# A causal convolution and a Fourier layer on one core: full-height products in the second stage, and other buffers first for the mixing weights

## The chip, the cores and the metric

The kernel runs on one core of a Trainium2 chip. The metric is the device time of one execution in microseconds. Engines are named as in the profile: PE is TensorE (PEld its weight loads), DVE VectorE, ACT ScalarE, POOL GpSimd, SP SyncE.

## What is computed

`x` is 8 batches x 3264 rows x 192 channels (f32). First a causal convolution of 7 taps with softmaxed weights for each of 8 heads; its result is the `x` of the second part, a Fourier layer: the lowest 64 frequencies along the rows are mixed over the channels with complex matrices, transformed back and added to `x`, and then a small matrix product with a relu is added.

```python
out = np.einsum('hk,bskhg->bshg', w, x_unf)          # convolution, w = softmax(weight)
x = out.reshape(B, S, D)
...
X = np.fft.rfft(x, axis=1)                            # n_modes = 64
Yr = np.einsum('bmd,mde->bme', Xr, w_r) - np.einsum('bmd,mde->bme', Xi, w_i)
Yi = np.einsum('bmd,mde->bme', Xr, w_i) + np.einsum('bmd,mde->bme', Xi, w_r)
y = np.fft.irfft(Y, n=S, axis=1)
u = x + y
return (u + np.maximum(u @ w_ch, 0.0)).astype(np.float32)
```

## The kernel before, in words

The 8 batches form four pairs (`q` = 0 to 3). The convolved rows lie in `xall` (bf16) in slots of 128 rows of both batches of a pair: 25 whole slots and one of half tiles per pair. The order of the work on each engine is the order in which the program writes it; engines wait for each other by semaphores.

**First stage.** For each unit of four or five slots: convolution (`conv`, products of 64 rows and 64 columns of the array, L285), copies back to `xall` (L303, L305), and the product with the sine and cosine table `ftab` (`dft_unit`, full height, L311). Between them TensorE transposes the rows into `cm` (channels 0 to 127, `cm_bank`, L360) and `ct` (channels 128 to 191, two batches on the two halves of the partitions, `ct_bank`, L371); both are views of the tile `cc`, which has four quarters, one for each pair. `some(n)` does the next `n` of these banks from the list `tjobs`.

**Mixing.** 16 groups of four frequencies. `mix(g)` is 12 products (L428), each on a quarter of the array's columns, with the weights of group `g`. The weights come by GpSimd's queue (`load_w`, L417: two DMAs of 288 KB a group, for w_r and w_i). Nine groups have a place before the mixing starts: four in the last quarter of `cc`, which is still free, and five in the `arena`. `wbuf(g)` gives groups 0 to 3 the quarter of `cc` and 4 to 8 the arena; group `g` from 9 on goes where `g - 5` lay, and is loaded when `mix(g - 5)` is done. After each second group ScalarE copies the result out (`mix_copy`, L435), and TensorE transposes it (`mix_trans`, L441) into `yet` (copies L446, L448). Between the groups stand transposes of `ftab` and of the last quarter; those that write the last quarter of `cc` come after the groups whose weights lie there. The PSUM banks of the second stage's first two tiles (`za`) are taken after group 13, and the c products of the first two duos (`first_c`) run behind groups 13 and 14.

**Between.** `yet` is multiplied with `wm` and `w1` (L587, L588), which gives `zw`, the mixed frequencies with and without `w_ch`, for the first four batches; those of the others come in two items of the second stage (`zw_batch`, L505, L506).

**Second stage.** 53 items: 50 duos of two slots, one duo of half tiles ("h") and two items of `zw_batch`. Four PSUM tiles of two banks take turns (`za`, `zb`). What a duo adds up in PSUM:

- c: the rows times `w_ch`, from `cm` with `wm` and from `ct` with `wt2` (which holds the lower 64 rows of `w_ch` on both halves of the partitions);
- g: `ftab` times the part of `zw` that has `w_ch` in it; then a relu in place on ScalarE (`relu`, L521);
- y: `ftab` times the other part of `zw`; then VectorE adds `xall` (`finish`, L540) and SyncE stores the result (L549, 384 KB a duo).

`both` issues c, g or y for the two units of a duo side by side: one unit on rows 0 to 63 of the array, the other on rows 64 to 127, each into its own bank, and later with the halves exchanged. A bank takes the other half only when the first is done: `turn` puts a wait there. One duo has 20 products of half height, all at L499. An item `n` of the loop issues c and g of the first half for `n`, y of the second half for `n - 2` with its add and store, c and g of the second half for `n` and its relu, and y of the first half for `n - 1`.

Of the kernel before, what the change touches and what calls it, by code (L numbers as in the profile page):

```python
# [19 lines left out]
def kernel(  # L20
# [32 lines left out]
    def sb(name, shape, dtype, **kw):  # L53
# [5 lines left out]
    NW = 5  # L59
# [363 lines left out]
    def mix(g):  # L423
        yp = low[(g // 2) % 2][:, D * (g % 2):D * (g % 2) + D]
        for j in range(3):
            for p4 in range(4):
                m = 4 * g + p4
                nc.tensor.matmul(yp[32 * p4:32 * p4 + 2 * B, :], xt[:, j, :, m],  # L428
                                 wbuf(g)[:, p4, j, :], start=(j == 0), stop=(j == 2),
                                 tile_position=(0, 32 * p4), skip_group_check=True)  # L430
        if g >= NL:
            load_w(g + NW)

    def mix_copy(d):
        nc.scalar.copy(out=ymix[d % 2][:], in_=low[d % 2][:, 0:2 * D].rearrange("p (g d) -> p g d", g=2))  # L435

    def mix_trans(d):
        ets = [low[2 + t][:, :].bitcast(BF16)[:, 0:2 * P].rearrange("p (g k) -> p g k", g=2) for t in range(2)]
        for t in range(2):
            for g in range(2):  # L440
                nc.tensor.transpose(ets[t][:, g, :], ymix[d % 2][:, g, 64 * t:64 * t + P], ident[:])  # L441
        for t in range(2):
            dst = yet[:, t, :, :].rearrange("p (c m) b -> p m c b", c=2)[:, 8 * d:8 * d + 8, :, :]
            srcv = ets[t].rearrange("p g (q k) -> p (g q) k", q=4)[:, :, 0:16].rearrange("p m (c b) -> p m c b", c=2)
# [11 lines left out]
    some(2)  # L456


    def z_pieces(u, row, which):

        r = slice(64 * row, 64 * row + 64)
        res = []
        if u[0] == "h":
            for k, q in enumerate(u[1]):
                cols = slice(D * k, D * k + D)
                if which == "c":
                    res.append((cols, cm[r, q, 2 * NF, :], wm[r, 0:D]))
                    res.append((cols, ct[r, q, NF, :], wt2[r, :]))
                else:
                    for i in range(2):  # L470
                        res.append((cols, ftab[r, NF + i, :], zw[r, 2 * q + i, 0 if which == "g" else 1, :]))
        else:
            q, t = u
            if which == "c":
                for i in range(2):
                    res.append((slice(D * i, D * i + D), cm[r, q, 2 * t + i, :], wm[r, 0:D]))
                res.append((slice(D * row, D * row + D), ct[r, q, t, :], wt2[r, :]))
            else:
                res.append((slice(0, 2 * D), ftab[r, t, :],
                            zw[r, 2 * q:2 * q + 2, 0 if which == "g" else 1, :]))  # L480
        return res

    held = {}

    def both(duo, zt, first, which, begin=False, end=False):


        lists = (z_pieces(duo[first], 0, which), z_pieces(duo[1 - first], 1, which))
        old = held.get(id(zt))
        if old is not None and old[0] != first and not begin:  # L490
            turn(old[1])
        last = [None, None]
        for k in range(max(len(lists[0]), len(lists[1]))):
            for row in range(2):
                lst, bank = lists[row], first ^ row
                if k >= len(lst):
                    continue
                cols, l, r = lst[k]
                mm = nc.tensor.matmul(zt[:, bank, cols], l, r, start=(begin and k == 0),  # L499
                                      stop=(end and k == len(lst) - 1), skip_group_check=True)  # L500
                last[row] = mm.ins.name
        held[id(zt)] = (first, last)

    def zw_batch(b, zt, k):
        nc.tensor.matmul(zt[:, k, 0:2 * D], yet[:, 0, :, b], wm[:], start=True, stop=False)  # L505
# [17 lines left out]
    def finish(n):  # L523
        duo, zt = items[n]
        o = outs[n % NO]
        if duo[0][0] == "h":
# [6 lines left out]
            for i in range(2):  # L533
# [3 lines left out]
                nc.sync.dma_start(out=dst, in_=o[r, :, :].rearrange("p k (a d) -> p (k a) d", a=2))  # L537
            return
        s = [slot(*u) for u in duo]
        nc.vector.tensor_tensor(out=o[:, :, :], in0=zt[:, :, 0:2 * D],  # L540
                                in1=xall[:, s[0]:s[1] + 1:s[1] - s[0], :, :].rearrange("p k i d -> p k (i d)"),
                                op=ALU.add)
# [25 lines left out]
    for g in range(NG):  # L568
        mix(g)
        if g % 2:  # L570
            mix_copy(g // 2)
        if g < NG - 3:
            some(1 if g < 10 else 2 if g < 11 else 3, NT * (NQ - 1) if g < NL - 1 else NT * NQ)
        elif g == NG - 3:
            some(99)
            ring_stack.close()
            stack, pp = psum_pool("pz0", "left")
            ctx.push(stack)
            assign({k: pp.tile([P, 2, 512], F32, tag=f"za{k}", name=f"za{k}") for k in (0, 1)})
        if g % 2:  # L580
            mix_trans(g // 2)
        if g == NG - 3:
            first_c(0)
        elif g == NG - 2:
            first_c(1)
    for b, z in enumerate((low[0], low[2], low[3], low[1])):
        nc.tensor.matmul(z[:, 0:2 * D], yet[:, 0, :, b], wm[:], start=True, stop=False)  # L587
        nc.tensor.matmul(z[:, 0:2 * D], yet[:, 1, :, b], w1[:], start=False, stop=True)  # L588
# [4 lines left out]
    assign({k: pp.tile([P, 2, 512], F32, tag=f"zb{k}", name=f"zb{k}") for k in (2, 3)})  # L593

    ahead = 2
    for n in range(N + 2):
        duo, zt = items[n] if n < N else (None, None)
        old = [items[n - k][0] if 0 <= n - k < N else None for k in range(3)]
        zq = isinstance(duo, int)
        if n < N:  # L600
            if zq:
                for i in range(2):
                    zw_batch(2 * duo + i, zt, i)
                zw_copy(2 * duo, 2, zt[:, :, 0:2 * D], True)
            else:
                if n >= ahead:
                    both(duo, zt, 0, "c", begin=True)
                both(duo, zt, 0, "g")
        if isinstance(old[2], tuple):
            both(*items[n - 2], 1, "y", end=True)  # L610
            finish(n - 2)
        if n < N and not zq:
# [4 lines left out]
        if isinstance(old[1], tuple):  # L617
            both(*items[n - 1], 0, "y")


# [28 lines left out]
```

## Time and profile before

| what | us |
|---|---|
| median of 3 runs (190.28 to 192.6) | 190.3 |
| profiled execution | 191.59 |
| its span, first to last instruction | 189.7 |
| first stage, to the last slot's transform | to 80 |
| mixing: first group, last group start | 81.7, 111.4 |
| first mode product of the second stage | 115.9 |
| last relu of the second stage starts | 181.8 |
| TensorE, VectorE, ScalarE, GpSimd busy | 154.9, 116.5, 94.2, 66.6 |
| mean granted TensorE clock (1 is full) | 0.948 |

The profile is one execution on the chip. Rows in order of time have the start, the duration, the engine and line, the operation, what it writes and reads, the shapes, how many instructions follow each other, and in brackets the idle time before with what ended it. A matmul's duration runs from its start to its modelled end and overlaps the next; what one costs in a stream is the distance to the start of the next. `64*128` ahead of the operand's shape means that the product uses 64 rows and 128 columns of the array.

### The profile page before, as it was taken

The page shows a single profiled execution, that of the slowest core. Times are in us where ns is not written, and L with a number is a line of the kernel's source. Part 1 is how long each engine was busy: PE and PEld are TensorE (multiplying, and loading weights), DVE is VectorE, ACT ScalarE, POOL GpSimd, SP SyncE. Part 2 cuts the span into 40 slices and gives each one's busy share as a digit, 9 for nine tenths or more (in the row PEclk, how much of TensorE's full clock was granted, in tenths as well). Part 3 has the DMA queues.
Part 4 walks back from the last instruction along what each step waited for, and adds up shares of the span by engine and source line. Part 5 has one row for each costly group of instructions (what it writes and reads, how often), then busy time and mean ns, then how long its engine had stood idle before and what let it go on. Part 6 is the DMA issues. An engine that isn't in the chain of part 4 may idle for free.

```text
span 189.7 us, 6202 instructions
## 1 busy us (share of the span) xinstructions
PE 154.9 (82%) x2687; PEld 102.3 (54%) x2687; DVE 116.5 (61%) x178; ACT 94.2 (50%) x129; POOL 66.6 (35%) x115
## 2 busy tenths in 40 slices
PE   0046579999999999898739749999999999999950
PEld 0023347766666756665427423666667566666620
DVE  4879555686677757464413302678575977777770
ACT  2066745545653553444523215566665666666630
POOL 7998899669557734105731000000000000000000
PEclk9999978999999999999985975999999999999997
DMA  5999999999999999995999920489986799999993
GB/s 55 147 188 189 190 173 178 191 191 192 189 190 178 178 203 207 206 207 81 199 196 205 206 46 0 152 271 363 304 274 223 225 362 323 328 325 324 327 327 133
DMA packets 63179, 40.07 MB, mean 211 GB/s; under 512 B 28848, under 2 KB 63152, under 8 KB 63152
## 3 DMA queue, kind: packets, MB, share of 16 engines
q0 software_dynamic: 36000, 19.59, 76.0%
q1 hardware_dynamic: 27152, 20.09, 31.7%
q8 instruction: 21, 0.34, 0.7%
q14 instruction: 6, 0.05, 0.1%
HBM read 39.20 MB, written 20.05 MB: 312 GB/s over the span
## 4 chain that ended last, share of the span: by engine, by line
PE 67%; DMA 13%; POOL 7%; issue 4%; DVE 4%; ACT 2%; POOLq 0%; DVEq 0%; ACTq 0%
PE zb L499 17%; PE za L499 16%; PE z L285 11%; PE low L311 9%; DMA arena<-in_moe_w_i_dram 6%; DMA arena<-in_moe_w_r_dram 4%; PE low L360 4%; POOL xall L140 4%; DMA xall<-in_x_dram 3%; PE low L371 3%; POOL arena L417 1%; PE low L324 1%; PE low L428 1%; DVE xall L305 1%; ACT za L521 1%
## 5 line engine op out<-in xcount | busy, mean ns | idle before, releaser
L285 PE MATMUL z<-xall,band 64*64 64x192 bf16 (+2 forms) x800 | 27.2, 265 | 17.5 <-DVE band L188 11.6
L140 POOL DMA_DIRECT2D xall<-in_x_dram x48 | 38.2, 810 | 7.0 <-DMA xall<-in_x_dram 5.0
L499 PEld LDWEIGHTS <-cc 64*128 64x128 bf16 x616 | 24.4, 94 | 21.2 <-PE za L499 7.3
L499 PE MATMUL za<-mixa,ftab 64*128 64x384 bf16 x208 | 32.7, 331 | 0.6 <-ACT za L521 0.3
L305 DVE CAST xall<-z 128x768 bf16<-128x768 f32 (+1 forms) x24 | 24.5, 1021 | 13.6 <-PE z L285 12.1
L540 DVE TENSOR_TENSOR arena<-za,xall 128x768 f32<-128x768 f32 x26 | 24.8, 956 | 10.8 <-PE za L499 4.5
L285 PEld LDWEIGHTS <-band 64*64 64x64 bf16 x800 | 18.1, 110 | 24.5 <-ACT band L186 12.0
L499 PE MATMUL zb<-mixa,ftab 64*128 64x384 bf16 (+1 forms) x224 | 31.2, 311 | 0.1
L303 ACT CAST xall<-z 128x768 bf16<-128x768 f32 (+1 forms) x24 | 20.4, 851 | 15.1 <-PE z L285 13.8
L540 DVE TENSOR_TENSOR arena<-zb,xall 128x768 f32<-128x768 f32 x24 | 22.9, 957 | 7.5 <-ACT za L521 4.0
L521 ACT ACTIVATE za<-za 128x768 f32<-128x768 f32 x26 | 20.7, 795 | 11.1 <-PE za L499 11.1
L521 ACT ACTIVATE zb<-zb 128x768 f32<-128x768 f32 x25 | 19.9, 795 | 12.3 <-PE zb L499 12.3
L499 PEld LDWEIGHTS <-ftab 64*128 64x128 bf16 x432 | 19.6, 94 | 4.2 <-issue 2.1
L311 PE MATMUL low<-xall,ftab 128*128 128x384 bf16 x100 | 21.6, 343 | 0.0
L499 PE MATMUL za<-wm,cc 64*128 64x192 bf16 x208 | 17.4, 245 | 0.2
L499 PE MATMUL zb<-wm,cc 64*128 64x192 bf16 x200 | 17.1, 248 | 0.4 <-DVE arena L529 0.3
L360 PEld LDWEIGHTS <-xall 128*128 128x128 bf16 x208 | 14.0, 103 | 3.2 <-issue 0.5
L340 DVE COPY cc<-low 128x1024 bf16<-128x1024 bf16 (+2 forms) x19 | 11.8, 620 | 4.4 <-PE low L360 2.3
L340 DVE COPY cc<-r 128x1024 bf16<-128x1024 bf16 (+2 forms) x10 | 6.0, 604 | 13.7 <-PE r L371 8.3
L338 ACT COPY cc<-low 128x1024 bf16<-128x1024 bf16 (+1 forms) x9 | 8.5, 941 | 11.4 <-PE low L371 5.1
L417 POOL DMA_DIRECT2D arena<-in_moe_w_r_dram x12 | 7.6, 632 | 17.1 <-PE low L428 10.4
L499 PE MATMUL za<-wt,cc 64*128 64x192 bf16 x104 | 12.8, 243 | 0.0
(104 smaller groups left out, 175.0 us busy)
## 6 DMA issues: line engine op xcount, KB each, us to landing
out_dram<-arena SPq DMA_DIRECT2D x46, 384.0 KB, 3.9
xall<-in_x_dram POOLq DMA_DIRECT2D x24, 192.0 KB, 8.1
xall<-in_x_dram POOLq DMA_DIRECT2D x16, 240.0 KB, 7.1
arena<-in_moe_w_r_dram POOLq DMA_DIRECT2D x12, 288.0 KB, 11.1
arena<-in_moe_w_i_dram POOLq DMA_DIRECT2D x12, 288.0 KB, 11.2
out_dram<-arena SPq DMA_DIRECT2D x10, 192.0 KB, 2.9
xall<-in_x_dram POOLq DMA_DIRECT2D x8, 144.0 KB, 7.0
cc<-in_moe_w_r_dram POOLq DMA_DIRECT2D x4, 288.0 KB, 7.2
```

The source lines that it names most:

```text
L140: nc.gpsimd.dma_start(out=xall[:, s0:s0 + nf, i, :], in_=src)
L285: mm = nc.tensor.matmul(ov[c], band[r, h, c.start + shift + 64 * (r is UP and c is LO): c.start + shift + 64 * (r is UP and c is LO) + 64] ...
L303: nc.scalar.copy(out=dst, in_=srcv)
L305: nc.vector.tensor_copy(out=dst, in_=srcv)
L311: nc.tensor.matmul(xp, ftab[:, t, :], xall[:, slot(q, t), :, :], start=(t == 0), stop=False, skip_group_check=True)
L338: nc.scalar.copy(out=out, in_=in_)
L340: nc.vector.tensor_copy(out=out, in_=in_)
L360: nc.tensor.transpose(tp[:, P * k:P * k + P], xall[:, slot(q, t), i, 0:P], ident[:])
L417: nc.gpsimd.dma_start(out=wbuf(g)[64 * half:64 * half + 64, :, :, :], in_=src[4 * g:4 * g + 4, :, :].rearrange("m (p j) e -> p m j e", j=3))
L499: mm = nc.tensor.matmul(zt[:, bank, cols], l, r, start=(begin and k == 0), stop=(end and k == len(lst) - 1), skip_group_check=True)
L521: nc.scalar.activation(out=zt[:, :, 0:2 * D], in_=zt[:, :, 0:2 * D], func=ACT.Relu)
L540: nc.vector.tensor_tensor(out=o[:, :, :], in0=zt[:, :, 0:2 * D], in1=xall[:, s[0]:s[1] + 1:s[1] - s[0], :, :].rearrange("p k i d -> p k (i ...
```

## The change

There are five parts.

1. **Second stage at full height.** c products from `cm` (`heads`) and the g and y products (`modes`) are no longer split into halves of 64 rows: each is one product over 128 rows, for one bank. The c products from `ct` and `wt2` (`tails`) stay at 64 rows, two units side by side, then exchanged. A duo has 12 products instead of 20. The turns remain between the first and second set of tails, and between the tails and the heads. For the half tiles all products are of full height. An item of the loop issues: second tails of `n`, y for `n - 2`, heads of `n`, first tails of `n + 1`, g for `n`.
2. **Buffers.** Groups 0 to 4 lie in the arena, 5 to 8 in the last quarter of `cc`. Group `g` from 9 to 13 is loaded when `mix(g - 9)` is done, 14 and 15 when `mix(9)` and `mix(10)` are.
3. **Order of the mixing.** The first group stands ahead of the transposes of `ftab`. The transposes that write the last quarter of `cc` start at group 8. How many banks follow each group stands in `PLAN`. All are done before the last group.
4. **Around the last group.** The last pair of groups is copied and transposed in two halves, the first one ahead of `mix(15)`. The c products of duos 0 and 1 stand behind `mix(15)`.
5. **Last store.** The last duo is added and stored in two halves, the second from ScalarE's queue.

```diff
-           for a, n in ((late, NL), (arena, NW)) for i in range(n)]
+           for a, n in ((arena, NW), (late, NL)) for i in range(n)]
 
     def wbuf(g):
-        return wts[g] if g < NL else wts[NL + (g - NL) % NW]
+        return wts[g] if g < NW + NL else wts[(g - NW - NL) % NW]
...
-        if g >= NL:
+        if g < NW:
+            load_w(g + NW + NL)
+        elif g >= NW + NL:
             load_w(g + NW)
...
+    def tails(n, first):
+        duo, zt = items[n]
+        if duo[0][0] == "h":
...
+        if first:
+            turn(order[n])
+        names = []
+        for row in range(2):
+            bank = row ^ first
+            q, t = duo[bank]
+            r = slice(64 * row, 64 * row + 64)
+            mm = nc.tensor.matmul(zt[:, bank, D * row:D * row + D], ct[r, q, t, :], wt2[r, :], start=(first == 0),
+                                  stop=False, skip_group_check=True)
+            names.append(mm.ins.name)
+        order[n] = names
+
+    def heads(n):
+        duo, zt = items[n]
+        turn(order[n])
+        for k, u in enumerate(duo):
+            for j in range(2):
+                cols = slice(D * j, D * j + D)
+                product(n, k, cols, cm[:, u[1][j], 2 * NF, :] if u[0] == "h" else cm[:, u[0], 2 * u[1] + j, :],
+                        wm[:, 0:D])
+
+    def modes(n, which):
...
+                product(n, k, slice(0, 2 * D), ftab[:, t, :], zw[:, 2 * q:2 * q + 2, which, :], stop=(which == 1))
...
+        if n == N - 1:
+            for k, (q, t) in enumerate(duo):
+                nc.vector.tensor_tensor(out=o[:, k, :], in0=zt[:, k, 0:2 * D],
+                                        in1=xall[:, s[k], :, :].rearrange("p i d -> p (i d)"), op=ALU.add)
...
+                eng = nc.scalar if k else nc.sync
+                eng.dma_start(out=dst, in_=o[:, k, :].rearrange("p (i d) -> p i d", i=2))
+            return
...
     def first_c(n):
-        for first in range(2):
-            both(*items[n], first, "c", begin=(first == 0))
+        tails(n, 0)
+        tails(n, 1)
+        heads(n)
...
+    PLAN = (1, 1, 1, 1, 1, 1, 1, 1, 1, 2, 2, 2, 1, 2, 99)
+    for g in range(NG - 1):
         mix(g)
-        if g % 2:
+        if g == NG - 2:
+            mix_copy(g // 2, slice(0, 1))
+        elif g % 2:
             mix_copy(g // 2)
...
+    mix(NG - 1)
+    mix_copy(NG // 2 - 1, slice(1, 2))
+    first_c(0)
+    mix_trans(NG // 2 - 1, slice(1, 2))
+    first_c(1)
...
     for n in range(N + 2):
...
+        if tiles(n):
+            if n > ahead and n - 1 < N and not tiles(n - 1):
+                tails(n, 0)
+            if n >= ahead:
+                tails(n, 1)
...
+        if tiles(n - 2) and n >= 2:
+            modes(n - 2, 1)
             finish(n - 2)
...
+        if tiles(n):
             if n >= ahead:
-                both(duo, zt, 1, "c")
-            both(duo, zt, 1, "g")
-            relu(zt)
+                heads(n)
+            if tiles(n + 1) and n + 1 >= ahead:
+                tails(n + 1, 0)
+            modes(n, 0)
+            relu(items[n][1])
```

Three places on TensorE show what moves; rows that repeat the one above are left out. The first is the middle of the second stage, from one duo into the next. Before, all products at L499 are of half height; `cc` with `wm` and `wt2` are the c products, `ftab` with `mixa` the modes (`zw` lies in the tile `mixa`):

```order
L499 LDWEIGHTS cc_60 [waits PE_49]
L499 MATMUL zb3_2136<-wm_65,cc_60 128x192
L499 MATMUL zb3_2136<-wt2_67,cc_60 128x192
L499 MATMUL zb3_2136<-mixa_63,ftab_61 128x384
L499 MATMUL zb2_2135<-mixa_63,ftab_61 128x384 [waits Activation_49]
L499 MATMUL za0_2054<-wm_65,cc_60 128x192 [waits DVE_49]
L499 MATMUL za0_2054<-wt2_67,cc_60 128x192
L499 MATMUL za0_2054<-mixa_63,ftab_61 128x384
```

In the change, L485 are tails of 64 rows and L466 products of 128 rows:

```order
L485 LDWEIGHTS cc_60 [waits PE_49]
L485 MATMUL zb3_2133<-wt2_67,cc_60 128x192
L466 MATMUL za1_2078<-mixa_63,ftab_61 128x384 [waits Activation_49]
L466 LDWEIGHTS cc_60 [waits PE_49]
L466 MATMUL zb3_2133<-wm_65,cc_60 128x192
L485 MATMUL za0_2077<-wt2_67,cc_60 128x192 [waits DVE_49]
L466 MATMUL zb3_2133<-mixa_63,ftab_61 128x384
```

The two sets of tails of a duo now stand on either side of the modes of the duo before, and each set of tails stands between products of full height. A wait for `PE_49` is a turn.

The second place is the end of the mixing, from the c products of duo 0 to the first product for `zw`. Before:

```order
L499 MATMUL za0_2054<-wt2_67,cc_60 128x192
L428 MATMUL low1_87<-arena_59,mixa_63 16x192 [waits DMASW2_49]
L499 MATMUL za1_2055<-wm_65,cc_60 128x192
L499 MATMUL za1_2055<-wt2_67,cc_60 128x192
L428 MATMUL low1_87<-arena_59,mixa_63 16x192 [waits DMASW4_49]
L441 LDWEIGHTS ymix1_75 [waits Activation_49]
L441 MATMUL low3_89<-ident_68,ymix1_75 128x128
L587 LDWEIGHTS yet_62 [waits DVE_49]
```

And now:

```order
L444 MATMUL low3_89<-ident_68,ymix1_75 128x128
L428 MATMUL low1_87<-arena_59,mixa_63 16x192 [waits DMASW4_49]
L485 MATMUL za0_2077<-wt2_67,cc_60 128x192 [waits Activation_49]
L466 MATMUL za0_2077<-wm_65,cc_60 128x192
L444 LDWEIGHTS ymix1_75 [waits Activation_49]
L485 MATMUL za1_2078<-wt2_67,cc_60 128x192
L466 MATMUL za1_2078<-wm_65,cc_60 128x192
L608 LDWEIGHTS yet_62 [waits DVE_49]
```

The c products of both duos have moved behind the wait for the last weights (`DMASW4_49`), and half of the transposes ahead of it.

The third place is the start of the mixing. Before:

```order
L326 MATMUL low2_88<-perm_69,xs1_73 64x128
L352 MATMUL r0_1610<-ident_68,ftab_61 128x128
L352 MATMUL r1_1611<-ident_68,ftab_61 128x128
L428 MATMUL low0_86<-cc_60,mixa_63 16x192 [waits DMASW6_49]
L352 MATMUL r2_1612<-ident_68,ftab_61 128x128
```

And now:

```order
L326 MATMUL low2_88<-perm_69,xs1_73 64x128
L428 MATMUL low0_86<-arena_59,mixa_63 16x192 [waits DMASW6_49]
L352 MATMUL r0_1610<-ident_68,ftab_61 128x128
L428 MATMUL low0_86<-arena_59,mixa_63 16x192 [waits DMASW0_49]
L352 MATMUL r1_1611<-ident_68,ftab_61 128x128
```

The first group has moved ahead of two banks of `ftab`, and its weights lie in the arena instead of `cc`.

More of the change, by code (lines that the diff above doesn't have):

```diff
@@ L455 @@
     tjobs = [(0, g_bank, 8 * k, min(8, NTM - 8 * k)) for k in range((NTM + 7) // 8)] + tjobs
[L456 to L469, printed above, removed]
-                    for i in range(2):
[L471 to L477, printed above, removed]
-            else:
-                res.append((slice(0, 2 * D), ftab[r, t, :],
-                            zw[r, 2 * q:2 * q + 2, 0 if which == "g" else 1, :]))
-        return res
@@ L483 @@
[L483 to L502, printed above, removed]
+    order = {}
@@ new lines, in product @@
+    def product(n, bank, cols, l, r, start=False, stop=False):
+        mm = nc.tensor.matmul(items[n][1][:, bank, cols], l, r, start=start, stop=stop, skip_group_check=True)
+        return mm.ins.name
+    def tails(n, first):
+        duo, zt = items[n]
+        if duo[0][0] == "h":
+            if first == 0:
+                order[n] = [product(n, k, slice(D * j, D * j + D), ct[:, q, NF, :], wt2[:, :], start=(j == 0))
+                            for k, u in enumerate(duo) for j, q in enumerate(u[1])]
+            return
[10 more added lines that the diff above has]
+        order[n] = names
```

71 lines of the change are left out of this document (34 added, 37 removed).

## The prediction

> **What bounds the kernel now.** I read the chain of the work that ended last first, then the windows by stage, then the second stage and the mixing on TensorE in order of time.
>
> ```profile
> PE 67%; DMA 13%; POOL 7%; issue 4%; DVE 4%; ACT 2%; POOLq 0%; DVEq 0%; ACTq 0%
> ...
> L521 ACT ACTIVATE za<-za 128x768 f32<-128x768 f32 x26 | 20.7, 795 | 11.1 <-PE za L499 11.1
> ```
>
> Two thirds of the chain are TensorE. ScalarE's relu of the second stage waits for TensorE every time. The next fence is the window from 150 to 180 us, in the second stage (columns: stretch, length, busy time of PE, PEld, DVE, ACT, POOL, granted clock, DMA share, GB/s).
>
> ```profile
> 150.00:180.00 30.00, 30.00 (x494) 19.71 (x492) 23.56 (x25) 19.71 (x25) 0.00 (x0) 1.00 0.99 328
> ```
>
> TensorE has no free time, VectorE and ScalarE have a fifth and a third left, and the stores keep the DMA engines at a share of 0.99. So the pitch of the second stage is TensorE's. One duo, the unit of that stage, in order of time:
>
> ```profile
> 161.00 0.33 PE L499 MATMUL za<-wm,cc 64*128 64x192 bf16 x4
> 161.16 0.25 PE L499 MATMUL za<-wt,cc 64*128 64x192 bf16 x2
> 161.24 0.33 PE L499 MATMUL za<-mixa,ftab 64*128 64x384 bf16 x2
> 161.41 0.33 PE L499 MATMUL zb<-mixa,ftab 64*128 64x384 bf16 x2
> 161.63 0.34 PE L499 MATMUL za<-wm,cc 64*128 64x192 bf16 x4
> 161.81 0.24 PE L499 MATMUL za<-wt,cc 64*128 64x192 bf16 x2
> 161.89 0.33 PE L499 MATMUL za<-mixa,ftab 64*128 64x384 bf16 x2
> 162.06 0.33 PE L499 MATMUL zb<-mixa,ftab 64*128 64x384 bf16 x2
> 162.22 0.25 PE L499 MATMUL za<-wm,cc 64*128 64x192 bf16 x2
> ```
>
> 162.22 - 161.00 = 1.22 us a duo. A pair of half-height products side by side takes 0.08 us for 192 columns (161.16 to 161.24) and 0.163 for 384 (161.24 to 161.41). Six short and four long pairs make 1.14 us; the missing 0.08 stands at 161.41 to 161.63 and just after, where the second set of c products waits for its turn on the bank.
>
> **The second stage in the change.** A full-height product replaces a pair, so the columns that stream stay the same: four heads of 192, two pairs of tails of 192, four mode products of 384, again 1.14 us. The stall goes too: from the start of the last product to the release of a turn that waits for it are 0.39 us at 384 columns (161.24 to 161.63), so 0.31 at the 192 of a tail, and between a tail and what waits for it now lie two mode products, 2 x 0.163 + 0.08 = 0.41 us. So far the change saves 0.08 us a duo. But the tails stay half-height, because the two halves of wt2 meet two different units. Now TensorE goes tails, modes and heads, tails, modes: four changes between 64 rows and 128 rows in every duo, where before it made none. What such a change costs is in the trace at two places, the zw products in the second stage and the first stage:
>
> ```profile
> 139.98 0.49 PE L499 MATMUL zb<-mixa,ftab 64*128 64x384 bf16 x4
> 140.40 0.38 PE L505 MATMUL za<-wm,yet 128*128 128x384 bf16 x1
> ...
> 140.78 0.33 PE L505 MATMUL za<-wm,yet 128*128 128x384 bf16 x1
> 140.95 0.33 PE L506 MATMUL za<-w,yet 128*128 128x384 bf16 x1
> 141.21 0.50 PE L499 MATMUL zb<-mixa,ftab 64*128 64x384 bf16 x4
> ```
>
> ```profile
> 45.41 0.82 PE L311 MATMUL low<-xall,ftab 128*128 128x384 bf16 x4
> 46.07 0.61 PE L360 MATMUL low<-ident,xall 128*128 128x128 bf16 x8
> ...
> 47.63 0.82 PE L311 MATMUL low<-xall,ftab 128*128 128x384 bf16 x4
> 48.39 0.64 PE L371 MATMUL low<-ident,xall 128*64 128x128 bf16 x16
> ```
>
> Half to full height: two pairs last 0.33, but 139.98 to 140.40 is 0.42, so 0.09 more. Back to half: 140.95 to 141.21 is 0.26, against 0.17 from 140.78 to 140.95, again 0.09. In the first stage four products followed by the same tile shape take 0.66 (45.41 to 46.07), followed by another shape 0.76 (47.63 to 48.39): 0.10. It is the same in both directions and for each shape, with nothing to wait for. I take 0.10 with the slower second product behind each change. Pitch: 1.14 + 4 x 0.10 = 1.54 us, 0.32 more than now. The stage has 53 items; without the first two, the two zw items with the one behind each, and the half tiles, 46 regular duos are left: 46 x 0.32 = 14.7. Behind each zw item the two sets of tails stand together: two changes (0.20) and a bare turn (0.31 - 0.08) against the old stall of 0.08, 0.35 each, 0.7 for both. **Sum +15.4 us.** Bounds of one change are 0.09 (the lowest row) and 0.12 (0.10 and the 0.02 by which products start slower behind a stall, 161.63 to 161.81 against 161.00 to 161.16): pitch 1.50 to 1.62, +13.6 to +19.1. At 1.54 the other engines have more air than now (relu 0.80, DVE add 0.96), and the DMA share falls to 0.99 x 1.22 / 1.54 = 0.78, so nothing of it hides behind another engine.
>
> The Trainium skill, TensorEngine Tiling (Array Packing), Key Properties, says that changing the tiling mode, not just the tile, drains TensorE. It gives no time; with the drain of some 128 cycles, 0.053 us, that TensorE: Matmul & The Clock Gate gives in its step-by-step section, the pitch would be 1.35 us and the kernel some 194 us, an estimate from those pages. The rows above show nearly twice that, and the rows decide.
>
> **The weights.** The stretch where the mixing begins, with GpSimd's first reload:
>
> ```profile
> 86.00:87.00 1.00, 0.52 (x12) 0.42 (x16) 0.89 (x2) 0.51 (x3) 0.00 (x0) 1.00 0.62 105
> 87.00:88.00 1.00, 1.00 (x40) 0.78 (x32) 0.15 (x2) 0.18 (x1) 0.42 (x1) 1.00 0.09 15
> 88.00:89.00 1.00, 0.69 (x19) 0.39 (x11) 0.56 (x1) 0.67 (x2) 1.00 (x3) 1.00 0.28 27
> 89.00:90.00 1.00, 1.00 (x28) 0.67 (x30) 0.43 (x3) 0.35 (x2) 1.00 (x3) 1.00 0.76 90
> 90.00:110.00 20.00, 13.90 (x240) 9.77 (x232) 5.90 (x17) 6.18 (x12) 6.15 (x11) 0.83 1.20 201
> ```
>
> ```profile
> 81.68 0.46 PE L428 MATMUL low<-cc,mixa 128*16 128x192 bf16 x12
> ...
> 87.58 0.61 POOL L417 DMA_DIRECT2D arena<-in_moe_w_r_dram  x1 [10.37 <-PE low L428]
> ```
>
> GpSimd waits 10.37 us for mix(4), because group 9 goes where group 4 lay. Against a share of 1.20 the DMA engines lose 0.58 + 1.11 + 0.92 + 0.44, divided by 1.20: 2.5 us. With the arena first, group 9 needs only mix(0), which ran at 81.68 and stands ahead of the ftab transposes now, 4 to 5 us before the queue runs dry. Groups 14 and 15 wait for mix(9) and mix(10), a group or more ahead of need. Behind the waiting load on GpSimd's queue are only later loads. So the last weights come 2.5 us earlier. Below nothing: no loss, since the order of the bytes is the same.
>
> **After the last weights.** Here the change adds work to the path.
>
> ```profile
> 108.48 0.46 PE L428 MATMUL low<-arena,mixa 128*16 128x192 bf16 x12 [0.48 <-DMA arena<-in_moe_w_i_dram]
> 108.87 0.34 PE L499 MATMUL za<-wm,cc 64*128 64x192 bf16 x4
> ...
> 111.36 0.46 PE L428 MATMUL low<-arena,mixa 128*16 128x192 bf16 x12 [1.58 <-DMA arena<-in_moe_w_i_dram]
> ...
> 113.18 0.54 PE L587 MATMUL low<-wm,yet 128*128 128x384 bf16 x1
> ...
> 115.89 2.52 PE L499 MATMUL za<-mixa,ftab 64*128 64x384 bf16 x10
> ```
>
> Before, from mix(15) to the first zw product 1.82 us pass. The first c products of duos 0 and 1 were done while the last two groups were on their way. Now they come behind mix(15): 0.39 to the first (108.48 to 108.87), 0.31 for each of two turns, 0.33 for four heads, so 0.95 a duo; with the transposes between, 2.5 us at full clock, 0.7 more than now. At half clock it is some 3.9, 2.1 more. The clock decides:
>
> ```profile
> 98.30:105.10 6.80, 5.41 (x76) 4.32 (x76) 1.67 (x4) 2.48 (x4) 1.22 (x2) 0.51 1.21 206
> 105.10:111.90 6.80, 3.89 (x76) 2.15 (x72) 1.52 (x6) 1.01 (x3) 0.00 (x0) 0.99 0.90 153
> 111.90:118.70 6.80, 5.94 (x30) 2.58 (x32) 1.46 (x3) 3.50 (x6) 0.00 (x0) 0.51 0.00 0
> ```
>
> A stretch that was 80% busy (5.41 of 6.80) was followed by a clock of 0.99, one at 57% by 0.51, and that half clock lay over all the zw products and the start of the second stage. In the change TensorE works without a break from mix(15) on, so that stretch should be some 70% busy, between the two. With full clock the zw products and the start gain about 2.2 us (eight products at 0.16 instead of 0.32, and the pipeline's fill): front -2.5 + 0.7 - 2.2 = -4.0. With half clock the gain is eaten: -2.5 + 2.1 + 0.3 = -0.1. As neither row is nearer, I take the middle: **-2.0 us**, bounds -4.0 and -0.1.
>
> The Trainium skill, TensorE: Matmul & The Clock Gate, has the clock fall after a window of idle TensorE ("No PE-idle gaps >~3µs between matmul bursts" in its table of goals). By that the clock would stay full here, and the time would be 2 us lower. The trace does not agree: 105.1 to 111.9 had no such gap (108.87 to 111.36 holds products and is shorter) and yet 0.51 followed.
>
> **The end.**
>
> ```profile
> 183.49 0.96 DVE L540 TENSOR_TENSOR arena<-za,xall 128x768 f32<-128x768 f32 x1
> ...
> SPq L644 <- DMA out_dram<-arena: 3.4, 1, 3.4
> ...
> out_dram<-arena SPq DMA_DIRECT2D x10, 192.0 KB, 2.9
> ```
>
> The last store of 384 KB is waited for 3.4 us after its issue, behind full queues. Now a half of 192 KB is last, 2.9 at most, and the queues are at 0.78; DVE's two halves together take as long as the one add. **-1.0 us**, between -0.5 and -1.5.
>
> **Sum.** +15.4 - 2.0 - 1.0 = +12.4 us. The profiled execution took 191.59 us with a span of 189.7: that becomes 204.0 and 202.1. Against the median of the runs, 190.3, it is **202.7 us**.
>
> **The rivals.**
> Hidden changes (the other side): the next shape's weights are loaded under the running products, as those of the same shape are, and the changes cost nothing. Pitch 1.14: 46 x -0.08 = -3.7, with -3.0 for front and end 183.6 us; the stores would need a share of 0.99 x 1.22 / 1.14 = 1.06, under the 1.20 of the weights. It decides from a change below 0.02 us on. For it: the modes around a tail depend on nothing late. Against it: neither did the products around 141.21. 8%.
> Half price: two of the four changes fall together with a turn's or a bank's wait, 0.05 each on the mean, pitch 1.34: 46 x 0.12 + 0.3 - 3.0 = +2.8, 193.1 us. Against it: those waits end before the change does (0.31 against 0.41). 6%.
> No gain in front: half clock, and the transposes of the last quarter, now later in the mixing, hold the last groups up; front +0.5, 205.2 us. 14%.
> The clock falls in the second stage, since TensorE streams only 1.14 of 1.54 us (74%, between the 57% and the 80% above). Two stretches of 6.8 us at half clock have a pitch of 2 x 1.14 + 0.4 = 2.7 and lose 1.9 duos of 1.54 each: +5.8 with the rest as forecast, 208.5 us. 6%.
> The forecast itself: 66%.
>
> **How the numbers follow.** The forecast's own range is 199 to 207 (pitch 1.50 to 1.62, front -4.0 to -0.1). Downward it takes in nothing of the two cheap cases (14%), upward all of the no-gain case: 198 to 207.5. A measurement tells about 2% (3.8 us) from no change. Faster by more: the hidden changes, 0.08; within: half price, 0.06; slower: the rest, 0.86.
>
> **What would show it.** In the changed profile: relus 1.54 us apart, no wait longer than 0.1 us between tails and what follows, 0.09 to 0.10 more than the stream at each change; DMA share near 0.78 in the second stage; GpSimd's wait for the mixing gone and mix(15) near 108.8 us; a first zw product 2.5 to 4 us behind it. The prediction falls if the pitch is under 1.3 us, or if the second stage starts later than 116 us.

## The result and the profile after

| | before | the change |
|---|---|---|
| median of the runs | 190.84 us (4 runs) | 203.56 us (4 runs, 202.59 to 204.41) |
| ratio | | 1.065, 95% interval 1.056 to 1.074 |
| profiled execution, own time | 191.59 us | 203.81 us |
| its span | 189.7 us | 202.0 us |
| third relu starts | 119.71 us | 118.11 us |
| third relu to last relu | 62.10 us | 77.17 us |
| last relu to the end of the span | 7.9 us | 6.7 us |

The kernel is 6.5% slower. Ratios and intervals compare the means of the runs without those that took over 1.5% longer than the fastest of the same kernel, and medians take in all runs. The three last rows cut the span at two relus of the second stage: -1.60 us in front, +15.07 us inside the stage, -1.2 us at the end, together the 12.3 us by which the span grew.

The two relus in the kernel before, from ScalarE's work in order of time (start, duration, what ended its wait):

```profile
119.71 0.80 ACT L521 ACTIVATE zb<-zb 128x768 f32<-128x768 f32 x1 [1.03 <-PE zb L499]
...
181.81 0.80 ACT L521 ACTIVATE za<-za 128x768 f32<-128x768 f32 x1 [0.43 <-PE za L499]
```

In the changed kernel, the third relu and those at the end of the stage:

```profile
118.11 0.80 ACT L528 ACTIVATE zb<-zb 128x768 f32<-128x768 f32 x1 [0.82 <-PE zb L466]
...
192.44 0.80 ACT L528 ACTIVATE zb<-zb 128x768 f32<-128x768 f32 x1 [0.78 <-PE zb L466]
194.01 0.80 ACT L528 ACTIVATE zb<-zb 128x768 f32<-128x768 f32 x1 [0.78 <-PE zb L466]
195.28 0.80 ACT L528 ACTIVATE za<-za 128x768 f32<-128x768 f32 x1 [0.48 <-PE za L466]
```

194.01 - 192.44 = 1.57 us a duo, against 1.22 before. The last duo takes 1.27: no tails of a later item stand among its modes, so it has 0.08 us less to stream and two changes of height less, 0.30 us together. That difference alone prices a change at 0.11 us.

The window from 150 to 180 us (columns as in the prediction), and the chain of the work that ended last, by engine:

```profile
150.00:180.00 30.00, 29.81 (x232) 14.93 (x230) 19.15 (x20) 14.68 (x20) 0.00 (x0) 1.00 0.74 245
```

```profile
PE 43%; DMA 10%; issue 1%; POOL 1%; ACT 1%; DVE 0%; DVEq 0%; POOLq 0%
```

The chain goes back to 82 us only. TensorE makes up 43% of the span in it, and from 116 us to the last relu it consists of TensorE's products but for less than 1 us.

In the window TensorE still counts as busy for 29.81 of 30 us, but only 20 relus of ScalarE fall into it, one for each duo, where there were 25. The column of busy time does not show the loss; the starts of the products do. One duo on TensorE, in order of time:

```profile
159.89 0.49 PE L466 MATMUL zb<-wm,cc 128*128 128x192 bf16 x4
160.32 0.26 PE L485 MATMUL zb<-wt,cc 64*128 64x192 bf16 x2
160.50 0.50 PE L466 MATMUL zb<-mixa,ftab 128*128 128x384 bf16 x2
160.94 0.26 PE L485 MATMUL zb<-wt,cc 64*128 64x192 bf16 x2
161.12 0.50 PE L466 MATMUL za<-mixa,ftab 128*128 128x384 bf16 x2
161.46 0.49 PE L466 MATMUL zb<-wm,cc 128*128 128x192 bf16 x4
```

161.46 - 159.89 = 1.57. Two modes followed by heads of the same height take 0.34 (161.12 to 161.46); two modes followed by tails take 0.44 (160.50 to 160.94): 0.10 for the change down. A pair of tails streams in 0.08 and takes 0.18 (160.32 to 160.50, 160.94 to 161.12): 0.10 for the change up. The weight loads at the second of these changes:

```profile
160.93 0.10 PEld L485 LDWEIGHTS <-cc 64*128 64x128 bf16 x2 [0.32 <-PE zb L485]
161.12 0.11 PEld L466 LDWEIGHTS <-ftab 128*128 128x128 bf16 x2
161.30 0.43 PEld L466 LDWEIGHTS <-cc 128*128 128x128 bf16 x4
```

The load for the heads starts at 161.30, 0.16 us ahead of its products (161.46), under the running mode. The load for the tails and the one for the modes behind them start with their own products (160.93 with 160.94, 161.12 with 161.12): across these changes of height no load runs ahead.

The view of waits, from 120 to 194 us, would lead a reader elsewhere (columns: us in total, times, longest):

```profile
PEld L485 <- issue: 7.7, 47, 0.3
PEld L485 <- PE za L485: 7.2, 23, 0.3
PEld L485 <- PE zb L485: 6.6, 21, 0.3
```

These three rows, 21.5 us together, are idle time of the weight loads ahead of tails, and nearly two thirds of it are booked on the turn, for which the second tails wait. The first experiment tells whether the turn or the change of height costs that.

### The profile page after: what moved, and what is told of

Same layout as the page of the kernel before. It is cut to its first block, busy times and chain, and to the rows that moved or that the text cites. A ratio compares the mean times of both kernels' runs of the same rounds, so it can differ in the third digit from the quotient of the medians.

```text
span 202.0 us, 5363 instructions
## 1 busy us (share of the span) xinstructions
PE 168.6 (83%) x2263; PEld 100.8 (50%) x2263; DVE 116.9 (58%) x180; ACT 94.0 (47%) x131; POOL 66.9 (33%) x115
## 4 chain that ended last, share of the span: by engine, by line
PE 43%; DMA 10%; issue 1%; POOL 1%; ACT 1%; DVE 0%; DVEq 0%; POOLq 0%
PE za L466 15%; PE zb L466 15%; DMA arena<-in_moe_w_i_dram 10%; PE za L485 5%; PE zb L485 5%; POOL arena L417 1%; PE low L428 1%; PE low L608 1%; PE low L609 0%; ACT za L528 0%; ACT mixa L518 0%; PE r L360 0%; PE r L371 0%; DVE arena L550 0%; DVEq L667 0%
## 5 line engine op out<-in xcount | busy, mean ns | idle before, releaser
L557 DVE TENSOR_TENSOR arena<-za,xall 128x768 f32<-128x768 f32 x25 | 23.9, 958 | 17.0 <-PE za L466 16.5
L466 PE MATMUL za<-mixa,ftab 128*128 128x384 bf16 x104 | 25.9, 331 | 0.6 <-ACT za L528 0.6
L466 PE MATMUL zb<-mixa,ftab 128*128 128x384 bf16 (+1 forms) x112 | 25.6, 319 | 0.0
L466 PEld LDWEIGHTS <-cc 128*128 128x128 bf16 x208 | 18.8, 99 | 7.0 <-PE za L485 0.8
L485 PEld LDWEIGHTS <-cc 64*128 64x128 bf16 x200 | 9.8, 93 | 24.5 <-issue 8.5
L466 PEld LDWEIGHTS <-ftab 128*128 128x128 bf16 x216 | 13.3, 97 | 9.9 <-issue 0.8
L360 PEld LDWEIGHTS <-xall 128*128 128x128 bf16 x208 | 13.4, 100 | 3.5 <-issue 0.6
L485 PE MATMUL za<-wt,cc 64*128 64x192 bf16 x104 | 13.6, 259 | 0.2
L466 PE MATMUL za<-wm,cc 128*128 128x192 bf16 x104 | 13.5, 255 | 0.2
L485 PE MATMUL zb<-wt,cc 64*128 64x192 bf16 x96 | 12.3, 252 | 0.5 <-ACT mixa L518 0.3
## 6 DMA issues: line engine op xcount, KB each, us to landing
arena<-in_moe_w_r_dram POOLq DMA_DIRECT2D x12, 288.0 KB, 10.2
arena<-in_moe_w_i_dram POOLq DMA_DIRECT2D x12, 288.0 KB, 11.2
```

What stands on the lines that cost most here:

```text
L360: nc.tensor.transpose(tp[:, P * k:P * k + P], xall[:, slot(q, t), i, 0:P], ident[:])
L466: mm = nc.tensor.matmul(items[n][1][:, bank, cols], l, r, start=start, stop=stop, skip_group_check=True)
L485: mm = nc.tensor.matmul(zt[:, bank, D * row:D * row + D], ct[r, q, t, :], wt2[r, :], start=(first == 0), stop=False, skip_group_check=True)
```

## The experiments

Ratios are to the kernel before, with 95% intervals; the pitch is the distance of two relus in the regular part of the second stage. Edits are against the change where nothing else is said.

**One height throughout.** The tails of a unit become one product of 128 rows; turns and order stay. Part of the tails' result is left out.

```diff
-        names = []
-        for row in range(2):
...
-        order[n] = names
+        q, t = duo[first]
+        order[n] = [product(n, first, slice(0, D), ct[:, q, t, :], wt2[:, :], start=True)]
```

> The tails of a unit become one product over all 128 rows and 192 columns, so that no product of the second stage uses half the rows; order, turns and counts of columns stay. It computes the tails only for half of the columns, and adds up the channels of both batches there: that part of the result is left out. Theory (each change between 64 and 128 rows costs about 0.10 us, four per duo): pitch 1.14 to 1.16 us instead of 1.57, time near 184 us. Rival (the turns and the new order cost it): pitch stays near 1.57, time near 203.

Measured: 184.78 us, 0.972 [0.962, 0.983]. TensorE and ScalarE in order of time in this kernel:

```profile
160.92 0.25 PE L466 MATMUL za<-wt,cc 128*128 128x192 bf16 x1
161.00 0.49 PE L466 MATMUL zb<-mixa,ftab 128*128 128x384 bf16 x2
161.33 0.25 PE L466 MATMUL za<-wt,cc 128*128 128x192 bf16 x1
161.41 0.49 PE L466 MATMUL zb<-mixa,ftab 128*128 128x384 bf16 x2
161.73 0.49 PE L466 MATMUL za<-wm,cc 128*128 128x192 bf16 x4
162.06 0.25 PE L466 MATMUL za<-wt,cc 128*128 128x192 bf16 x1
```

```profile
167.25 0.80 ACT L521 ACTIVATE za<-za 128x768 f32<-128x768 f32 x1 [0.35 <-PE za L466]
168.40 0.80 ACT L521 ACTIVATE za<-za 128x768 f32<-128x768 f32 x1 [0.35 <-PE za L466]
```

The pitch is 1.145 us, the bare stream. The turns are still there and cost nothing. So it is not the turn that the view of waits names, but the change of height beside it. The stores reached a DMA share of 1.03 here (150 to 175 us) without holding the stage up.

**Tails together, behind the modes.** Two changes a duo, and one turn with nothing in front of it.

```diff
-            if n > ahead and n - 1 < N and not tiles(n - 1):
-                tails(n, 0)
             if n >= ahead:
+                tails(n, 0)
                 tails(n, 1)
...
-            if tiles(n + 1) and n + 1 >= ahead:
-                tails(n + 1, 0)
```

> Both sets of tails of a duo stand together at the start of its item, with a bare turn between them: two changes of height per duo instead of four, and one uncovered wait of 0.31 - 0.08 = 0.23 us. Theory: 1.57 - 0.20 + 0.23 = 1.60 us a duo, time within 1.5 us of the change's 203.6, near 205. Rival (waits cost, changes are free): 1.57 + 0.23 = 1.80 us a duo, time near 214.

Measured: 204.39 us, 1.076 [1.065, 1.086].

```profile
171.85 0.80 ACT L528 ACTIVATE za<-za 128x768 f32<-128x768 f32 x1 [0.80 <-PE za L466]
173.44 0.80 ACT L528 ACTIVATE zb<-zb 128x768 f32<-128x768 f32 x1 [0.80 <-PE zb L466]
```

The pitch is 1.597 us, taken over more duos than the two rows show. Less the stream of 1.145 and the bare turn's 0.23 (0.31 to the release, less the 0.08 of the tails themselves), 0.22 are left for two changes, 0.11 each. The rival, by which waits cost and changes are free, wanted 1.80. Fewer changes did not help, since the turn that had been hidden came out: 0.23 instead of 2 x 0.1.

**Six changes.** The two products of the first tails are parted by a mode product.

```diff
-            if tiles(n + 1) and n + 1 >= ahead:
-                tails(n + 1, 0)
-            modes(n, 0)
...
+                for row in range(2):
+                    tail(n + 1, row)
+                    q, t = duos[n][row]
+                    product(n, row, slice(0, 2 * D), ftab[:, t, :], zw[:, 2 * q:2 * q + 2, 0, :])
```

> The two products of the first tails are parted by one of the two mode products: six changes of height per duo instead of four; the two tails no longer run side by side (0.08 us). Same result, same turns. Theory: 1.57 + 0.20 + 0.08 + 0.02 = 1.87 us a duo, time near 217. Rival (changes are free): 1.65 us a duo, time near 207.

Measured: 216.31 us, 1.138 [1.129, 1.148].

```profile
166.45 0.80 ACT L536 ACTIVATE zb<-zb 128x768 f32<-128x768 f32 x1 [1.06 <-PE zb L466]
168.31 0.80 ACT L536 ACTIVATE zb<-zb 128x768 f32<-128x768 f32 x1 [1.06 <-PE zb L466]
```

The pitch is 1.859 us, 0.289 more. A tail that stands alone no longer shares its 0.08 with the other, which makes 0.08; the other 0.21 are two changes of 0.104. With 0, 4 and 6 changes a duo the pitch is 1.145, 1.570 and 1.859: 0.106 and 0.104 a change.

**One height by block weights.** Each set of tails is one product of 128 rows and 384 columns, with the halves of `wt2` as the diagonal blocks of a weight tile and zeros beside them; the turns fall away. It computes the whole result.

```diff
-        if first:
-            turn(order[n])
-        names = []
...
+        q, t = duo[first]
+        order[n] = [product(n, first, slice(0, 2 * D), ct[:, q, t, :], wd[:, :], start=True)]
```

> The tails of a unit become one product of 128 rows and 384 columns with a weight tile that holds the 64 rows of w_ch twice, on the diagonal, and zeros beside: the full result, no product of half height in the second stage, and no turns, for 2 x 0.163 us instead of 2 x 0.08. Theory: 4 x 0.082 + 6 x 0.163 = 1.31 us a duo, 0.26 less than the change, time near 191.5, about that of the kernel before. Rival (full-height products themselves are slower than pairs of half ones, by their weight loads): pitch stays over 1.45, time over 198.

Measured: 190.0 us, 0.994 [0.988, 0.999], 10 runs.

```profile
166.79 0.80 ACT L523 ACTIVATE za<-za 128x768 f32<-128x768 f32 x1 [0.51 <-PE za L471]
168.09 0.80 ACT L523 ACTIVATE za<-za 128x768 f32<-128x768 f32 x1 [0.51 <-PE za L471]
```

Twice 0.08 us more to stream, no change of height: a pitch of 1.305 us instead of 1.570, and nearly 14 us back. It is still above the 1.22 of the half-height products of before.

**All parts but the second stage.** The half-height second stage of before, with the other parts of the change. Of the edit, only the heads of two functions are shown.

```diff
-    def tails(n, first):
...
+    def both(duo, zt, first, which, begin=False, end=False):
```

> The second stage of the kernel before (half height throughout), with all the other parts of the change: buffers, order of the mixing, c products behind the last group, last store in halves. Theory: the loss sits in the second stage alone, the rest gains 1.6 us up to the third relu and 1.0 at the end: pitch 1.22 us, time near 188.4 against 191.0 of before. Rival (the new mixing and its c products behind the last group cost as much as they gain): time near 191.

Measured: 189.2 us, 0.986 [0.979, 0.993], 10 runs. TensorE at the end of the mixing, then ScalarE:

```profile
107.39 0.69 PE L428 MATMUL low<-arena,mixa 128*16 128x192 bf16 x12 [0.99 <-DMA arena<-in_moe_w_i_dram]
...
110.99 0.54 PE L604 MATMUL low<-wm,yet 128*128 128x384 bf16 x1
```

```profile
116.42 0.80 ACT L525 ACTIVATE zb<-zb 128x768 f32<-128x768 f32 x1 [0.83 <-ACT za L525]
```

The third relu starts at 116.42 us, where it was 119.71, and from the last relu to the end 8.1 us pass, where it was 7.9: the gain lies in front, and none at the end. The other parts are a gain of 1.4% by themselves, or 1.1% by the medians (189.2 against 191.2 us). The loss of the change lies in its second stage alone.

**The same with the c products ahead of the last group.** The edit is against the last kernel.

```diff
+    first_c(0)
+    first_c(1)
     mix(NG - 1)
     mix_copy(NG // 2 - 1, slice(1, 2))
-    first_c(0)
     mix_trans(NG // 2 - 1, slice(1, 2))
-    first_c(1)
```

> As the kernel with the half-height stage and the rest of the change, but the c products of duos 0 and 1 ahead of the last mixing group instead of behind it. Theory: the first zw product follows the last group by 1.8 us instead of 3.8, time 1 to 2 us lower, near 187. Rival (they hold the last group up by as much, or a lower clock eats it): the same time as with them behind, near 188.4.

Measured: 188.37 us, 0.987 [0.979, 0.996], the same as the last.

```profile
109.81 0.46 PE L428 MATMUL low<-arena,mixa 128*16 128x192 bf16 x12
111.22 0.39 PE L604 MATMUL low<-wm,yet 128*128 128x384 bf16 x1 [0.23 <-DVE yet L451]
```

The first zw product now comes 1.41 us behind the last group instead of 3.60, but the last group starts 2.42 us later: 111.22 against 110.99, the same time, as the rival had it. The two profiles do not show why, since more than the order differs. The last weights were issued at 98.10 us here and at 96.18 in the kernel without this edit, and landed some 11.2 us later in both, at 109.3 and 107.35; the c products held the last group up for the remaining 0.5 us. And the zw products ran at full clock here (0.16 us from one to the next) and most of them at half clock there (0.32).

**The weight buffers alone**, on the kernel before.

```diff
-           for a, n in ((late, NL), (arena, NW)) for i in range(n)]
+           for a, n in ((arena, NW), (late, NL)) for i in range(n)]
...
-        return wts[g] if g < NL else wts[NL + (g - NL) % NW]
+        return wts[g] if g < NW + NL else wts[(g - NW - NL) % NW]
...
-        if g >= NL:
+        if g < NW:
+            load_w(g + NW + NL)
+        elif g >= NW + NL:
             load_w(g + NW)
```

> The kernel before with the arena's buffers first and the reloads from the first group on, and the transposes into the last quarter from group 8 on; nothing else. Theory: GpSimd's wait of 10 us is gone, the last group comes 2.4 us earlier, time 2.0 to 2.5 us lower, near 188.7. Rival (the transposes, now later, hold the last groups up): less than 1 us lower.

Measured: 187.88 us, 0.987 [0.979, 0.994]. GpSimd's first reload, the DMA share a little later, and the last group:

```profile
83.78 0.61 POOL L417 DMA_DIRECT2D arena<-in_moe_w_r_dram  x1 [6.24 <-PE low L428]
```

```profile
88.00:89.00 1.00, 1.00 (x32) 0.77 (x29) 0.31 (x2) 0.27 (x1) 0.69 (x2) 1.00 1.21 206
```

```profile
108.23 0.69 PE L428 MATMUL low<-arena,mixa 128*16 128x192 bf16 x12 [0.89 <-DMA arena<-in_moe_w_i_dram]
```

GpSimd still waits 6.24 us, but the reload is issued at 83.78 instead of 87.58 us, the share stays at 1.21 where it had fallen to 0.28, and the last group starts 3.1 us earlier. This one edit beats the kernel before by 2.6 us [1.1, 4.0], and the change by far. The two versions before it, which hold the moves at the end of the mixing as well, are no better.

**The halved last store alone**, on the kernel before.

```diff
+        if n == N - 1:
...
+                eng = nc.scalar if k else nc.sync
+                eng.dma_start(out=dst, in_=o[:, k, :].rearrange("p (i d) -> p i d", i=2))
+            return
```

> The kernel before with the last duo's add and store in halves; nothing else. Theory of the forecast: 0.5 to 1.0 us lower, near 190.2. Rival (the queue is still full of the stores before it, since the stage runs at a DMA share of 0.99, so the end stays): the same time, 191.0, and in the change the gain at the end came from the emptier queue.

Measured: 190.69 us, 0.999 [0.994, 1.004], 10 runs. The two halves in its view of the DMA issues (from 181.5 us on; KB each, us from issue to landing):

```profile
out_dram<-arena SPq DMA_DIRECT2D x1, 192.0 KB, 3.8
out_dram<-arena ACTq DMA_DIRECT2D x1, 192.0 KB, 3.9
```

No gain: each half took 3.8 to 3.9 us to land, by either queue, as long as the whole last store of the kernel before (3.9).

**The change without the halved store.**

```diff
-        if n == N - 1:
...
-                eng.dma_start(out=dst, in_=o[:, k, :].rearrange("p (i d) -> p i d", i=2))
-            return
```

> The change with its last store whole again (one add, one store of 384 KB from SyncE's queue). Theory, from the profiles so far: in the change the last half goes by ScalarE's queue and lands 2.9 us after its issue, a whole store in the light queue lands after 2.6, and the two half adds last 1.02 us, the whole one 0.96: the same time within 0.5 us, near 203.5, and the gain at the end is the emptier queue's. Rival (the forecast's term): the halves are worth 0.5 us or more, last relu to the end of the span 7.2 us or more instead of 6.7.

Measured: 203.66 us, 1.071 [1.062, 1.080], the same as the change. In its profile the whole store was waited for 2.9 us (3.4 before), and 7.1 us passed from the last relu to the end: 0.8 less than before, with no halves. This last store took 3.4 us to land, and not the 2.6 of the median that was expected.

**The change with the c products ahead of the last group.**

```diff
+    first_c(0)
+    first_c(1)
     mix(NG - 1)
     mix_copy(NG // 2 - 1, slice(1, 2))
-    first_c(0)
     mix_trans(NG // 2 - 1, slice(1, 2))
-    first_c(1)
```

> The change with the c products of duos 0 and 1 ahead of the last mixing group instead of behind it. Theory, from the pair of kernels with the half-height stage: the last group starts up to 1 us later and the zw products follow it 2 us sooner, so the second stage starts 0 to 1 us earlier, time near 203. Rival (the forecast's 2.1 us at half clock is a loss that comes back in full): time near 201.5.

Measured: 203.5 us, 1.065 [1.054, 1.075], the same as the change. In its profile the last weights landed at 108.4 us, but the last group started behind the c products at 111.37, and the first zw product 1.69 us behind it, at 113.06; in the change these two were at 108.98 and 112.80. From the landing of the last weights to the first zw product 4.6 us passed here and 3.9 in the change: ahead of the last group the c products cost at least what they save behind it.

## Why the prediction held, point by point

**What bounds the kernel: right.** The regular part of the second stage follows TensorE's pitch, from 1.145 to 1.859 us in the kernels above, and the other engines and the stores never set it there.

**The stream and the stall: right.** The bare stream was put at 1.14; the kernel of one height has 1.145, with the turns hidden behind the two modes as forecast.

**The price of a change: right, and it carried the result.** Taken at 0.10 from places where the kernel before changed its tile shape; measured 0.096 down and 0.105 up, and 0.011 for the second product behind each change up. The pitch was 1.57 for 1.54. The page TensorEngine Tiling (Array Packing) of the Trainium skill, Key Properties, has TensorE drain at a change of tiling mode; the runs agree that a change costs time, but the 0.053 us that the prediction worked out beside it from TensorE: Matmul & The Clock Gate is half of what they show. Whether the 0.1 us are a drain, or the load that is no longer hidden, or both, the runs do not tell apart.

**The count of duos: off, and made up for.** The prediction took 46 regular duos. Between the third and the last relu are 48 intervals, and 36 of them are regular: 36 x 0.348 = 12.5 us. The other 12 (around the two zw items, the half tiles, the first and the last) went from 18.11 to 20.66 us, +2.5, since some of them hold two changes of height and not four. A price that was too low (36 x 0.028 = 1.0 us) and a count that was too high (1.4 us) left 15.07 for the 15.4 forecast.

**The weights: right.** -2.38 us for -2.5 (the last group at 108.98 instead of 111.36); alone, the edit is worth 2.6 us [1.1, 4.0]. That the single profiles come so close is luck: with the same mixing code the last group started between 106.84 and 108.98 us in seven kernels, and with that of before at 110.15 in the kernel of the halved store. One sign to look for was wrong: GpSimd's wait is not gone.

```profile
83.05 0.61 POOL L417 DMA_DIRECT2D arena<-in_moe_w_r_dram  x1 [4.75 <-PE low L428]
...
86.00:90.00 4.00, 3.14 (x64) 2.23 (x63) 1.82 (x5) 2.28 (x5) 1.96 (x4) 1.00 1.21 206
```

GpSimd still waits 4.75 us, but the share is 1.21 throughout: what counts is whether the queue runs dry, not whether the engine that feeds it waits.

**After the last weights: the value near, in part by luck, its reason half.** From the last group to the first zw product 3.82 us passed, where the prediction had 1.82 and 2.1 more for the half clock, 3.9.

```profile
97.40:104.20 6.80, 3.88 (x82) 2.85 (x82) 1.51 (x3) 2.05 (x4) 0.61 (x1) 1.00 1.21 206
104.20:114.40 10.20, 8.65 (x79) 4.99 (x78) 2.63 (x9) 2.72 (x9) 0.00 (x0) 0.50 0.34 58
114.40:118.00 3.60, 3.33 (x24) 1.63 (x22) 1.45 (x2) 2.63 (x4) 0.00 (x0) 0.99 0.00 0
```

The prediction asked what a stretch from the last group on, some 70% busy, would be followed by. The half clock had begun at 104.2, ahead of the last group, behind a stretch that was 57% busy, as in the kernel before, and it ended at 114.4, in time for the modes. So the c products and five of the eight zw products ran at half clock, and the start of the second stage at the full one: neither of the two cases, and near the middle that was taken (-1.60 for -2.0). The size is not firm: up to there the kernel of the halved store has the code of before, and its third relu started at 117.47 us, ahead of the change's 118.11. The page TensorE: Matmul & The Clock Gate of the Trainium skill has, in its table of goals, the clock fall after a window of idle TensorE; here the longest idle time ahead of the fall was 1.88 us.

```profile
103.24 0.46 PE L428 MATMUL low<-arena,mixa 128*16 128x192 bf16 x12 [1.88 <-DMA arena<-in_moe_w_i_dram]
```

The forecast's finer point, what it costs to have the c products behind the last group, cannot be settled from single profiles, since the start of the last group moves so much. The medians say that their place costs or saves nothing that can be measured.

**The end: the size right by luck, its reasons not shown.** -1.2 us for -1.0. The prediction gave it to the halves and to the emptier queue. The halves of the change took as long to land, by either queue, as the whole store ahead of them (the last three stores, from 197 us on):

```profile
out_dram<-arena SPq DMA_DIRECT2D x1, 384.0 KB, 2.9
out_dram<-arena SPq DMA_DIRECT2D x1, 192.0 KB, 2.8
out_dram<-arena ACTq DMA_DIRECT2D x1, 192.0 KB, 2.9
```

What differs is how the last store runs out. Here are windows of the kernel before, of the change and of the one with the tails together (the last two columns are the DMA share and GB/s):

```profile
186.70:188.00 1.30, 0.00 (x0) 0.00 (x0) 0.00 (x0) 0.00 (x0) 0.00 (x0) 0.57 0.07 23
...
199.90:200.20 0.30, 0.00 (x0) 0.00 (x0) 0.00 (x0) 0.00 (x0) 0.00 (x0) 0.50 0.14 44
200.30:201.90 1.60, 0.00 (x0) 0.00 (x0) 0.00 (x0) 0.00 (x0) 0.00 (x0) 0.50 0.00 0
...
200.40:201.70 1.30, 0.00 (x0) 0.00 (x0) 0.00 (x0) 0.00 (x0) 0.00 (x0) 0.50 0.07 24
```

Before, the store ended with some 1.4 us at a share of 0.07, about one of the 16 DMA engines; in the change that lasted 0.4 us. It lasted 0.4 us with the whole store too, and again 1.4 with the tails together and with six changes, which have the halves and a stage as light on the queue as the change's, and whose ends took 7.6 us. So 1.0 us of the 1.2 goes with this lag of one DMA engine; between kernels with the long lag, 0.3 us (7.9 to 7.6) are left for the halves and the emptier queue together. Nor is that firm: with the c products first, the same end took 7.3 us at the short lag. What makes the engine lag is not shown.

**The rivals.** Hidden changes (a pitch of 1.14) came only in the kernel without changes, half price (1.34) not at all. Of the case of no gain in front, the half clock came, but not the late last groups. The clock stayed at 1.00 in the second stage, though TensorE streams there for 73% of the time (1.145 of 1.57).

**The range.** Its upper end does not follow from its terms: 190.3 + 19.1 - 0.1 - 0.5 is 208.8 us, and not 207.

## What to carry to other kernels

Ahead of a rewrite that mixes products of different heights in one loop, count the changes of tile shape in a turn of the loop and price each by a place of the same profile where such a change stands already: four at 0.1 us outweighed here a stall of 0.08 us that was removed. Keep one shape through the loop, even with zeros in the weights, where that streams less than the changes cost, and read the loss from the starts of the products, since busy time hides it and the view of waits books it on a semaphore that is not to blame. Time the parts of a change one by one: 1.4% were to be had from the buffers alone.

## What the runs showed of the hardware

- The clock was at half for 10.2 us while TensorE counted as busy for 85% of them (8.65 us).
- Half the bytes did not land sooner: at the end of the change the last whole store of 384 KB took 2.9 us, the two halves of 192 KB 2.8 (SyncE's queue) and 2.9 (ScalarE's); in the kernel of the halved store it was 4.0, 3.8 and 3.9.
- The last store ran out over about one DMA engine for 1.4 to 1.5 us in eight of the twelve profiles, and for 0.4 us in the other four. Both lengths came with halves and without, and both behind stages with a light queue (DMA share 0.65 to 0.74).
- The start of the last group moved by up to 2.1 us between executions of the same mixing code (106.84 to 108.98 us), so a microsecond in front can't be read from one profile.
